# Log-sum rows of a windowed attention: one product and a masked spread on VectorE, or four products and plain copies on ScalarE

## The chip, the cores and the metric

The kernel runs on one core of a Trainium2 chip. A core has TensorE (PE in the profile, its weight loads PEld), VectorE (DVE), ScalarE (ACT), GpSimd (POOL) and SyncE (SP, which only issues transfers here). The metric is the device time of one execution in microseconds; the median over several executions counts.

## The reference

Two attention layers over 2048 tokens with 1024 features and 32 heads of 32 features each, in float32. Layer A attends to 8 tokens at a stride of 2, layer B to the last 256 tokens. Their outputs stand side by side. Cut to layer B, which the change touches:

```python
qkv = (x @ wqkv).reshape(B, S, 3, H, Dh)          # S = 2048, H = 32, Dh = 32
scores = einsum("bhqd,bhkd->bhqk", q, k) * Dh ** -0.5
mask = (i - j >= 0) & (i - j < 256)
p = softmax(where(mask, scores, -1e9))
o = einsum("bhqk,bhkd->bhqd", p, v)
return o.reshape(B, S, D) @ wo
```

## The kernel before

**Units and groups.** The work is cut into 8 units of 512 tokens: four "dense" ones of layer B, then four of layer A. A unit has 8 groups of 4 heads, so there are 32 dense groups. Every float32 operand of the large products is split into a high fp32r part and the rest, and each product is three matmuls (high by high, high by rest, rest by high).

**Stages of a dense group** (`qk_items` and `attention`). The projections for q and k run on TensorE (L586), ScalarE and VectorE split the result (L523, L527), and transfers of SyncE stack the parts in `qst` and `kst`, on partitions 0 to 95. Partitions 96 to 127 are free for the log-sum. `first` (L1089) makes scores with queries on the partitions, 16 tiles a group (4 blocks of 128 queries by 4 heads); VectorE adds the mask and takes the maximum (L1094), ScalarE takes the exponential with its sum (L1099), whose result is thrown away. After 16 tiles `log_sum` takes the logarithm on ScalarE (L1112), and `parts` forms minus maximum minus logarithm on VectorE (L1117) and splits it into `hl`, 128 queries by 2 parts by 16 tiles (L1119, L1120). `rows` transposes `hl` on TensorE by a product with the identity (L1128). `spread` writes the rows into partitions 96 to 127 of `qst` (L1134). `second` (L1172) then makes the scores once more, transposed, over all 128 partitions: the extra rows subtract the log-sum, so that the exponential (L1179) gives finished probabilities in `pbuf`. Masks set what lies outside the window to zero, on GpSimd (L1158) or VectorE (L1161). `values` (L1219) multiplies with v.

**The rows before the change.** The product of L1128 has `hl` as weights, 128 by 32, and gives 32 rows of 128 queries: row 16a + 4j + b holds part a of head j in block b. `spread` runs once for each head j. It repeats these rows over the 4 blocks (32 by 512) and multiplies by `pick`, a pattern that keeps in block b only the rows 4j + b and 16 + 4j + b. In `kst`, partitions 96 to 127 hold ones for all heads (`ones`, L413, once at the start), so `second` sums the rows that `pick` has left.

**What sets the order.** Instructions are written out by a planner in the kernel. `Clock` holds an estimated time for each engine; `ck.use` adds an operation, `ck.defer` puts a function off until a planned time. A loop at the end (L1285 on) takes the item that can start first in TensorE's plan, out of four sequences: log-sum rows (`aux`), `second` and `values` (`twos`), `first` (`ones`), and the projections (`gemm`). On a tie that order decides. An item has an estimated cost on TensorE, 0.08 for the rows. The planner also chooses the engine: casts of weights (L218 ScalarE, L221 VectorE), evictions (L607, L610) and masks (L1158, L1161) go where its estimate ends first. So another estimate moves other instructions. On the chip each engine runs its list in the planner's order and waits on semaphores.

**Banks and buffers.** Scores and rows share four PSUM banks (`rs`), taken in turn; a bank is free again after L1099, L1179 or L1134. Projections have three banks (`rg`), the values one. `qst` and `kst` have two buffers each, for alternate groups. GpSimd also issues the loads of weights (L173), each after the VectorE split that frees its buffer.

Of the kernel before, what the change touches and what calls it, by code (L numbers as in the profile page):

```python
# [7 lines left out]
F32 = mybir.dt.float32  # L8
F32R = mybir.dt.float32r
AF = mybir.ActivationFunctionType  # L10
ALU = mybir.AluOpType
# [3 lines left out]
P = 128  # L15
# [28 lines left out]
BANK_LATE = 0.0  # L44
# [189 lines left out]
def kernel(ctx, tc, xs, wqk, wv, wo, outs, units):  # L234


    nc = tc.nc
# [10 lines left out]
    pickp = ctx.enter_context(tc.tile_pool(name="pickp", bufs=1))  # L248
# [9 lines left out]
    ck = Clock()  # L258
# [113 lines left out]
    qst = [stackp.tile([P, 4, S], F32R, tag=f"q{i}", name=f"qst{i}") for i in range(2)]  # L372
    kst = [stackp.tile([P, 4, 256 + S], F32R, tag=f"k{i}", name=f"kst{i}") for i in range(2)]

    cst = {}

    def constants():
        def bands(name, n, keep, fill, *conds):
            m = const.tile([P, n], F32, name=name) if isinstance(name, str) else name
            nc.gpsimd.memset(m, keep)  # L380
            for step, base, chan in conds:
                nc.gpsimd.affine_select(m, m, pattern=[[step, n]], compare_op=ALU.is_ge, fill=fill, base=base,
                                        channel_multiplier=chan)
            return m

        ident = cst["ident"] = const.tile([P, P], F32R, name="ident")
        keep = const.tile([P, P], F32, name="keep_d")
        nc.gpsimd.memset(keep, 0.0)
        nc.gpsimd.affine_select(ident, keep, pattern=[[-1, P]], compare_op=ALU.not_equal, fill=1.0, base=0,
                                channel_multiplier=1)  # L390
        pick = cst["pick"] = pickp.tile([32, 16], F32, name="pick")
        nc.gpsimd.memset(pick, 0.0)
        for row in (0, 16):
            nc.gpsimd.affine_select(pick, pick, pattern=[[-1, 16]], compare_op=ALU.not_equal, fill=1.0, base=-row,
                                    channel_multiplier=1)
        cst["mask_d"] = bands("mask_d", 384, 0.0, FAR, (1, -1, -1), (-1, 256, 1))
        near = cst["near"] = band0[:, :200].rearrange("p (v c) -> p v c", v=5)
        nc.gpsimd.memset(near, 0.0)
        for i in range(4):
            part = near[32 * i:32 * i + 32]  # L400
            for step, base, chan in ((1, -1, -1), (-1, 8, 1)):
                nc.gpsimd.affine_select(part, part, pattern=[[0, 5], [step, 40]], compare_op=ALU.is_ge, fill=FAR,
                                        base=base, channel_multiplier=chan)
        nc.gpsimd.affine_select(near[0:32, 0, :], near[0:32, 0, :], pattern=[[1, 40]], compare_op=ALU.is_ge, fill=FAR,
                                base=-8, channel_multiplier=0)
        cst["keep_f"] = bands("keep_f", P, BIG, 0.0, (-1, -1, 1))
        cst["keep_d"] = bands(keep, P, BIG, 0.0, (1, 0, -1))
        ck.use("pool", 3.0, ck.now)

        def ones():  # L410
            zero = cst["mask_d"][96:P, None, P:2 * P].to_broadcast([32, 24, P])
            for t in kst:
                nc.scalar.activation(t[96:P, :, :].rearrange("p j (a s) -> p (j a) s", s=P), zero, AF.Identity,  # L413
                                     bias=1.0, scale=1.0)
                ck.use("act", 2.7, ck.now)

        ck.defer(24.0, ones)

    pfree = [0.0]
# [7 lines left out]
    xt, xready, ot, rows, waiting = {}, {}, {}, {}, {}  # L427
# [24 lines left out]
    rg, rs, ro = Ring(psg, 7 - NS, "g"), Ring(pss, NS, "s"), Ring(pso, 1, "o")  # L452
# [7 lines left out]
    def latest(*ts):  # L460
        return None if any(t is None for t in ts) else max(ts)
# [420 lines left out]
    def x_items(u):  # L882
        xt[u], xready[u] = [], []

        def run(g):
            a, b = st.get(where["x", u, g])
            xt[u] += a
            xready[u] += b

        return [[(lambda: 0.0, lambda g=g: run(g), 0.0, lambda: None)] for g in range(4)]  # L890
# [175 lines left out]
    def attention(u, s):  # L1066
# [5 lines left out]
        q, kk = qst[buf], kst[buf]  # L1072
# [37 lines left out]
        def log_sum():  # L1110
            ln = small.tile([P, 16], F32, tag="ln", name="ln")
            nc.scalar.activation(ln, h["sm"], AF.Ln)  # L1112
            e = ck.use("act", 0.13, ck.now) - 0.03

            def parts():
                nl = small.tile([P, 16], F32, tag="nl", name="nl")
                nc.vector.tensor_tensor(nl, h["nm"], ln, op=ALU.subtract)  # L1117
                hl = small.tile([P, 2, 16], F32R, tag="hl", name="hl")
                nc.vector.tensor_copy(hl[:, 0, :], nl)  # L1119
                nc.vector.tensor_tensor(hl[:, 1, :], nl, hl[:, 0, :].bitcast(F32), op=ALU.subtract)  # L1120
                e2 = ck.use("dve", 0.52, e, port=True)
                aux.append(Item(lambda: latest(rs.when(BANK_LATE), e2), lambda: rows(hl), 0.08))

            ck.defer(e, parts)

        def rows(hl):
            ps, bank = rs.take()
            nc.tensor.matmul(ps[0:32, 0:P], hl.rearrange("p a b -> p (a b)"), cst["ident"], start=True, stop=True)  # L1128

            def spread():  # L1130

                h["rows"] = []
                for j in range(4):
                    nc.vector.tensor_tensor(q[96:P, j, :].rearrange("p (b s) -> p b s", s=P),  # L1134
                                            ps[0:32, None, 0:P].to_broadcast([32, 4, P]),
                                            cst["pick"][0:32, 4 * j:4 * j + 4, None].to_broadcast([32, 4, P]), op=ALU.mult)
                    e = ck.use("dve", 0.61, ck.now)
                    h["rows"].append(e + ROWS_LATE)
                rs.give(bank, e)

            return spread
# [102 lines left out]
    aux, ones, twos, gemm = [], [], [], []  # L1244
    for u in range(U):
        for s in range(NG):
            a, b = attention(u, s)
# [3 lines left out]
    for p in plan:  # L1251
        if p[0] == "qk":
            new = qk_items(p[1], p[2])
            if p == ("qk", 0, 0):
                q, k, x = new[:NK], new[NK:], x_items(0)
# [16 lines left out]
    gemm = [Item(r, lambda run=run, after=after: (run(), after)[1], c) for r, run, c, after in gemm]  # L1272

    ck.defer(0.0, constants)
    if WARM:
        idle = qst[1][:, 0, :]
        nc.vector.memset(idle.bitcast(F32), 0.0)
        ps, bank = rs.take()
# [6 lines left out]
    while True:  # L1285
# [3 lines left out]
        for name, seq in seqs.items():  # L1289
# [3 lines left out]
            t = seq[pos[name]].ready()  # L1293
# [4 lines left out]
        if ck.later and (best is None or ck.later[0][0] < best[0]):  # L1298
            t = ck.later[0][0]
# [3 lines left out]
        t, name = best  # L1303
# [52 lines left out]
```

## Time and profile before

| | |
|---|---|
| median of 3 runs | 1816.4 us (1812.44 to 1818.7) |
| the profiled execution | 1818.1 us |
| its span, first to last instruction | 1816.4 us |
| granted clock of TensorE, mean | 0.995 |
| L1128, product for the rows | 32, mean 223 ns |
| L1134, spread on VectorE | 128, mean 676 ns, 79.3 us busy |
| L1099, exponential of the first pass, 128 by 384 | 448, mean 557 ns |
| L586, projection products, 128 by 512 | 3072, 773.0 us busy |

A row of a group reads: line, engine, operation, result and operands, shapes and count, then busy time, mean duration and the idle time of that engine just before, with what ended it. In a list of waits stand the total in us, the number of waits and the longest. A product's duration runs from its start to its modelled end and overlaps the next one. All lines L are of the kernel before unless it is said otherwise; in the changed kernel the lines from 393 on have numbers up to four higher.

### The profile page before, as it was taken

To read this page: it belongs to the slowest core of one execution; us is meant where nothing else is said; L and a number is where in the kernel's file an instruction comes from. 1 tells how busy PE (TensorE), PEld (TensorE's weight loads), DVE (VectorE), ACT (ScalarE), POOL (GpSimd) and SP (SyncE) were. 2 spreads that over 40 slices of the span, in tenths; PEclk is the share of its full clock that TensorE was granted. 3 is DMA by queue.
4 is the path that set the end of the run, shared out by engine and by line. 5 is a ranking of instruction groups with operands and counts; after the bars stand their busy time and mean duration, and the time that the engine had idled before them with its cause. 6 is when DMAs were issued, how large, how long until landed. Compare 5 with 4: busy or idle time off the path is not lost.

```text
span 1816.4 us, 38617 instructions
## 1 busy us (share of the span) xinstructions
PE 1789.4 (99%) x14730; PEld 1465.3 (81%) x14730; DVE 1262.0 (69%) x2790; ACT 924.4 (51%) x2301; POOL 410.1 (23%) x950
## 2 busy tenths in 40 slices
PE   9999999999999999999999999999999999999999
PEld 6787878888777788778887788888888887888887
DVE  6677876768867769777677566646755766557866
ACT  5556466555655565656555344423542544446342
POOL 2313323222242223333224300101010011002220
PEclk9999999999999999999999999999999999999999
DMA  7354664544646555454545343536753674348984
GB/s 239 114 142 136 183 168 139 167 139 137 183 139 177 146 144 170 134 166 128 160 110 164 106 150 119 164 123 213 249 173 113 221 250 137 120 144 297 311 265 145
DMA packets 129241, 303.61 MB, mean 167 GB/s; under 512 B 16160, under 2 KB 31520, under 8 KB 129056
## 3 DMA queue, kind: packets, MB, share of 16 engines
q0 software_dynamic: 45216, 164.65, 28.7%
q1 hardware_dynamic: 73472, 116.56, 22.8%
q10 hardware_dynamic: 10368, 19.93, 3.0%
q8 instruction: 117, 1.92, 0.4%
q14 instruction: 68, 0.56, 0.1%
HBM read 189.79 MB, written 44.04 MB: 129 GB/s over the span
## 4 chain that ended last, share of the span: by engine, by line
PE 91%; DMA 3%; ACT 2%; DVE 2%; issue 1%; SPq 0%; POOL 0%; ACTq 0%; DVEq 0%; POOLq 0%
PE g L586 37%; PE g L654 18%; PE g L714 10%; PE g L773 8%; PE s L1172 5%; PE s L1089 5%; PE o L1219 5%; PE s L923 2%; PE o L984 2%; DMA r<-od 2%; DMA raw<-xs 1%; ACT wide L970 1%; ACT s L1099 0%; DVE w L224 0%; DVE r L846 0%
## 5 line engine op out<-in xcount | busy, mean ns | idle before, releaser
L586 PE MATMUL g<-x,w 128*128 128x512 f32 x3072 | 773.0, 396 | 2.8 <-ACT x L218 2.6
L586 PEld LDWEIGHTS g<-x,w 128*128 128x128 f32 x3072 | 568.1, 189 | 114.5 <-issue 6.8
L654 PE MATMUL g<-w,x 128*128 128x256 f32 (+1 forms) x2304 | 393.7, 322 | 0.5 <-issue 0.3
L224 DVE TENSOR_TENSOR w<-raw,w 128x512 fp32r<-128x512 f32 x518 | 339.4, 697 | 51.8 <-ACT w L218 45.1
L654 PEld LDWEIGHTS g<-w,x 128*128 128x128 f32 x2304 | 334.5, 192 | 28.8 <-issue 1.6
L1099 ACT ACTIVATE s<-s,nm 128x384 f32<-128x384 f32 (+2 forms) x512 | 274.4, 537 | 101.8 <-DVE nm L1094 101.6
L1094 DVE CUSTOM_DVE_ANT_0 s<-s,mask_d 128x384 f32<-128x384 f32 (+2 forms) x512 | 261.7, 554 | 88.1 <-PE s L1089 87.4
L1158 POOL TENSOR_SCALAR_AFFINE_SELECT pbuf<-pbuf 128x128 f32<-128x128 f32 (+1 forms) x606 | 220.1, 391 | 326.2 <-ACT pbuf L1179 324.8
L1179 ACT ACTIVATE pbuf<-s 128x384 f32<-128x384 f32 (+2 forms) x480 | 202.8, 505 | 73.7 <-PE s L1172 72.1
L714 PE MATMUL g<-r,w 128*128 128x512 f32 x768 | 190.8, 394 | 1.4 <-ACT r L1054 0.7
L173 POOL DMA_DIRECT2D raw<-wqk x126 | 68.6, 545 | 440.8 <-DVE w L224 303.0
L714 PEld LDWEIGHTS g<-r,w 128*128 128x128 f32 x768 | 141.9, 188 | 30.7 <-DVE r L1058 1.6
L773 PE MATMUL g<-x,w 128*128 128x512 f32 x672 | 153.2, 390 | 0.5 <-DVE w L224 0.5
L773 PEld LDWEIGHTS g<-x,w 128*128 128x128 f32 x672 | 126.0, 188 | 27.3 <-DVE w L224 0.9
L221 DVE CAST w<-raw 128x1024 fp32r<-128x1024 f32 x187 | 129.3, 692 | 25.2 <-PE g L586 22.6
L1172 PEld LDWEIGHTS s<-qst,kst 128*128 128x128 f32 x704 | 113.3, 189 | 40.6 <-ACT s L1099 16.2
L1089 PE MATMUL s<-kst,qst 96*128 96x384 f32 (+2 forms) x512 | 142.5, 342 | 0.9 <-ACT s L1099 0.7
L1172 PE MATMUL s<-qst,kst 128*128 128x256 f32 (+2 forms) x704 | 136.4, 302 | 3.5 <-ACT s L1099 3.0
L1089 PEld LDWEIGHTS s<-kst,qst 96*128 96x128 f32 x512 | 93.5, 189 | 25.8 <-issue 3.9
L931 DVE TENSOR_TENSOR band<-s,near 128x160 f32<-128x160 f32 x128 | 32.5, 316 | 116.0 <-PE s L923 116.0
L1099 ACT ACTIVATION_READ_ACCUMULATOR s<-s,nm 128x1 f32 x512 | 105.4, 206 | 0.0
L970 ACT COPY wide<-band 32x512 f32<-32x512 f32 x128 | 79.0, 618 | 49.2 <-DVE band L961 47.2
(81 smaller groups left out, 1405.7 us busy)
## 6 DMA issues: line engine op xcount, KB each, us to landing
raw<-wqk POOLq DMA_DIRECT2D x126, 512.0 KB, 4.3
raw<-wv POOLq DMA_DIRECT2D x72, 512.0 KB, 4.9
qst<-nat SPq DMA_DIRECT2D x96, 256.0 KB, 5.4
kst<-nat SPq DMA_DIRECT2D x96, 256.0 KB, 5.5
raw<-wo POOLq DMA_DIRECT2D x44, 512.0 KB, 4.4
raw<-xs POOLq DMA_DIRECT2D x28, 512.0 KB, 4.5
outs<-ost ACTq DMA_DIRECT2D x37, 256.0 KB, 2.8
kst<-halo SPq DMA_DIRECT2D x72, 128.0 KB, 4.4
```

What stands on the lines that cost most here:

```text
L221: nc.vector.tensor_copy(t[:, 0, :], raw)
L224: nc.vector.tensor_tensor(t[:, 1, c:c + 512], raw[:, c:c + 512], t[:, 0, c:c + 512].bitcast(F32), op=ALU.subtract)
L586: nc.tensor.matmul(h["ps"], h["w"][:, a, k * P:(k + 1) * P], xt[u][k][:, b, :], start=(k == 0 and i == 0), stop=(k == NK - 1 and i == 2))
L654: nc.tensor.matmul(ps, xt[u][kw * g + k][:, a, p0:p0 + P], h["w"][g][:, c, k], start=(first and t == 0 and half == 0), stop=(last and t == 2),
L714: nc.tensor.matmul(h["ps"], w[:, a, c:c + P], ot[u, k][:, b, :], start=(k == 0 and i == 0), stop=(k == NK - 1 and i == 2))
L773: nc.tensor.matmul(h["ps"], w[:, a, c:c + P], x[:, b, :], start=(k == 0 and t == 0), stop=(k == 3 and t == 2))
L1089: nc.tensor.matmul(ps[:, :n], q[0:96, j, b * P:(b + 1) * P], kk[0:96, j, c0:c1], start=True, stop=True)
L1094: nc.vector.tensor_tensor_reduce(ps[:, :n], ps[:, :n], mask[:, cut:full], scale=-1.0, scalar=BIG, op0=ALU.add, op1=ALU.min, accum_out=nm)
L1099: nc.scalar.activation(ps[:, :n], ps[:, :n], AF.Exp, bias=nm, scale=-1.0, accum_out=sm)
L1158: nc.gpsimd.affine_select(w, w, pattern=[[0, m], [step, n]], compare_op=ALU.is_ge, fill=0.0, base=base, channel_multiplier=chan)
L1172: nc.tensor.matmul(ps[:, i * n:(i + 1) * n], kk[:, j, 256 + kb * P:256 + (kb + 1) * P], q[:, j, q0:q0 + n], start=True, stop=True)
L1179: nc.scalar.activation(w, ps[:, :pack * n].rearrange("p (j n) -> p j n", j=pack), AF.Exp)
```

## The change

`pick` becomes a tile of 128 partitions; in its partitions 96 to 127 and first 4 columns it holds a one where the row is j or 4 + j in column j. The head's pattern is put into `kst` with it: `ones` adds column j of `pick` to zeros for head j, so only rows 96 + j and 100 + j are one there. Partitions 96 to 127 of both `qst` are set to zero once by GpSimd. `rows` makes four products, one for each block b, each with the 8 columns (part a, head j) of that block as weights; they fill 8 rows by 512 queries of one bank. `spread` copies these 8 rows to partitions 96 to 103 of `qst`, the same for each of the four heads, on ScalarE. The planner's costs change with it: 0.28 for the products, 0.485 on ScalarE for a copy in place of 0.61 on VectorE.

```diff
-        pick = cst["pick"] = pickp.tile([32, 16], F32, name="pick")
+        pick = cst["pick"] = pickp.tile([P, 16], F32, name="pick")
         nc.gpsimd.memset(pick, 0.0)
-        for row in (0, 16):
-            nc.gpsimd.affine_select(pick, pick, pattern=[[-1, 16]], compare_op=ALU.not_equal, fill=1.0, base=-row,
+        part = pick[96:P, :4]
+        for row in (0, 4):
+            nc.gpsimd.affine_select(part, part, pattern=[[-1, 4]], compare_op=ALU.not_equal, fill=1.0, base=-row,
                                     channel_multiplier=1)
...
         def ones():
-            zero = cst["mask_d"][96:P, None, P:2 * P].to_broadcast([32, 24, P])
-            for t in kst:
-                nc.scalar.activation(t[96:P, :, :].rearrange("p j (a s) -> p (j a) s", s=P), zero, AF.Identity,
-                                     bias=1.0, scale=1.0)
-                ck.use("act", 2.7, ck.now)
+            zero = cst["mask_d"][96:P, None, P:2 * P].to_broadcast([32, 6, P])
+            for t, qs in zip(kst, qst):
+                nc.gpsimd.memset(qs[96:P].bitcast(F32), 0.0)
+                ck.use("pool", 1.8, ck.now)
+                for j in range(4):
+                    nc.scalar.activation(t[96:P, j, :].rearrange("p (a s) -> p a s", s=P), zero, AF.Identity,
+                                         bias=cst["pick"][96:P, j:j + 1], scale=1.0)
+                    ck.use("act", 0.7, ck.now)
...
-                aux.append(Item(lambda: latest(rs.when(BANK_LATE), e2), lambda: rows(hl), 0.08))
+                aux.append(Item(lambda: latest(rs.when(BANK_LATE), e2), lambda: rows(hl), 0.28))
...
-            nc.tensor.matmul(ps[0:32, 0:P], hl.rearrange("p a b -> p (a b)"), cst["ident"], start=True, stop=True)
+            for b in range(4):
+                nc.tensor.matmul(ps[0:8, P * b:P * b + P], hl.rearrange("p a (j b) -> p a j b", b=4)[:, :, :, b],
+                                 cst["ident"], start=True, stop=True)
...
                 for j in range(4):
-                    nc.vector.tensor_tensor(q[96:P, j, :].rearrange("p (b s) -> p b s", s=P),
-                                            ps[0:32, None, 0:P].to_broadcast([32, 4, P]),
-                                            cst["pick"][0:32, 4 * j:4 * j + 4, None].to_broadcast([32, 4, P]), op=ALU.mult)
-                    e = ck.use("dve", 0.61, ck.now)
+                    nc.scalar.copy(q[96:104, j, :], ps[0:8, :])
+                    e = ck.use("act", 0.485, ck.now)
```

## The prediction

> **What bounds the kernel now.** I read the page first, then the busy time by stretches, then the waits of TensorE. The page: span, engines, chain.
>
> ```profile
> span 1816.4 us, 38617 instructions
> PE 1789.4 (99%) x14730; PEld 1465.3 (81%) x14730; DVE 1262.0 (69%) x2790; ACT 924.4 (51%) x2301; POOL 410.1 (23%) x950
> PE 91%; DMA 3%; ACT 2%; DVE 2%; issue 1%; SPq 0%; POOL 0%; ACTq 0%; DVEq 0%; POOLq 0%
> ```
>
> TensorE is the bound: busy for 99% of the span and 91% of the chain that ended last. VectorE, from which the change takes work, is 69% busy and makes 2% of the chain. The change touches the dense units alone, so I cut the span at the first scores and at the last log-sum row (columns: window, its length, then busy us of each engine, granted clock, DMA).
>
> ```profile
> 24.00:1015.00 991.00, 983.34 (x5966) 796.42 (x5965) 745.38 (x1926) 579.51 (x1676) 298.75 (x735) 1.00 0.54 152
> 1015.00:1816.40 801.40, 786.38 (x8706) 654.53 (x8704) 505.86 (x849) 336.05 (x612) 101.67 (x186) 1.00 0.56 185
> ```
>
> In the dense stretch TensorE is busy for 983.3 of 991.0 us: 7.7 us idle. ScalarE is 58% busy there (579.5/991), VectorE 75%. Whose fault the idle time is, the waits of TensorE in that window say; two waits of the weight loads and the first of ScalarE's follow.
>
> ```profile
> PE s L1172 <- ACT s L1099: 3.0, 4, 1.1
> PE s L1128 <- DVE hl L1120: 2.6, 3, 2.0
> PE s L1089 <- ACT s L1099: 0.7, 1, 0.7
> PE g L714 <- DVE r L1058: 0.5, 2, 0.2
> PE s L1172 <- ACT pbuf L1179: 0.3, 1, 0.3
> PE g L654 <- DVE w L224: 0.2, 1, 0.2
> ```
>
> ```profile
> PEld s L1172 <- ACT s L1099: 16.2, 26, 1.6
> ...
> PEld s L1128 <- ACT ln L1112: 3.8, 3, 2.4
> ```
>
> ```profile
> ACT s L1099 <- DVE nm L1094: 101.6, 104, 5.5
> ```
>
> Twelve waits, 7.3 us. The largest are for score banks that the exponentials (L1099) give back and for hl, the log-sum halves; none is for the spread rows of L1134. The weight loads wait 16.2 us for the same banks, most of it beneath a running product. ScalarE's exponentials themselves wait 101.6 us for VectorE's maxima. So all that a faster side engine can give back in the dense stretch is some 7 us and what hangs on it. One thing does: the longest wait, 2.0 us.
>
> ```profile
> 178.00:180.50 2.50, 0.51 (x4) 0.10 (x3) 1.22 (x4) 1.64 (x6) 0.00 (x0) 1.00 1.06 214
> 180.50:184.00 3.50, 3.50 (x17) 3.50 (x18) 3.22 (x6) 0.84 (x2) 0.00 (x0) 0.51 1.06 238
> ```
>
> Behind it the granted clock is 0.51 for 3.5 us, which costs 3.5 x 0.49 = 1.7 us more. Waits and clock: 9.0 us.
>
> **The change part by part: the products.** One product of 32 weight columns becomes four of 8, each with 128 moving columns, in 32 groups: 96 more products, all on TensorE, which has next to no idle time. Their price: the timeline at one of them, and the group of products with 128 moving columns and full weights.
>
> ```profile
> 465.25 0.22 PE L1128 MATMUL s<-ident,hl 128*32 128x128 f32 x1 [0.31 <-DVE hl L1120]
> 465.25 0.53 PEld L586 LDWEIGHTS g<-x,w 128*128 128x128 f32 x3
> 465.31 0.91 PE L586 MATMUL g<-x,w 128*128 128x512 f32 x3
> ```
>
> ```profile
> L1172 PE MATMUL s<-qst,kst 128*128 128x128 f32 x224 | 36.3, 260 | 2.2 <-ACT s L1099 1.8 <-ACT pbuf L1179 0.3
> ```
>
> The product is shown as 0.22 us long, but the next starts 0.06 us after it: products overlap, and what one takes of TensorE's time is that step. Three more a group: 3 x 0.06 x 32 = **5.8 us**, all on the path. From above: the 224 products with full weights are busy 36.3 us, 0.162 each, so 3 x 0.162 x 32 = 15.6 us; from below, 0, if every group's products fall into a wait that is there anyway. I take 5.8, since L1128 is the same product with the same moving operand, and eight weight columns are no more to load than 32.
>
> [...] The trace has a single product here and never four in a row, so no row settles it.
>
> **The spread.** The four VectorE instructions of a group go.
>
> ```profile
> L1134 DVE TENSOR_TENSOR qst<-s,pick 32x512 fp32r<-32x512 f32 x128 | 79.3, 676 | 9.9 <-PE s L1128 9.3
> ```
>
> VectorE loses 79.3 us. Four ScalarE copies from PSUM to an fp32r tile take their place, of 8 partitions and 512 elements. The rows nearest to them:
>
> ```profile
> L1054 ACT CAST r<-o 128x512 fp32r<-128x512 f32 x32 | 18.8, 587 | 38.5 <-PE o L1219 38.4
> L970 ACT COPY wide<-band 32x512 f32<-32x512 f32 x128 | 79.0, 618 | 49.2 <-DVE band L961 47.2
> L218 ACT CAST x<-raw 128x512 fp32r<-128x512 f32 x80 | 45.8, 618 | 53.6 <-DMA raw<-xs 21.5 <-DVE band L791 8.8 <-DMA outs<-ost 6.0
> L1179 ACT ACTIVATE pbuf<-s 128x512 f32<-128x512 f32 x112 | 65.1, 610 | 19.9 <-PE s L1172 18.7
> L1179 ACT ACTIVATE pbuf<-s 128x384 f32<-128x384 f32 x256 | 108.4, 507 | 38.6 <-PE s L1172 38.3
> ```
>
> ```profile
> 456.51 2.01 ACT L1179 ACTIVATE pbuf<-s 128x384 f32<-128x384 f32 x5
> ```
>
> A copy of 512 from PSUM takes 587 ns; 32 partitions (L970) cost the 618 of 128 (L218), so the 8 rows save nothing. In a row they overlap: five of 384 in 2.01 us step by (2.01 - 0.51)/4 = 0.38, and 512 add the 0.10 between 610 and 507: 0.48. A group's four last 3 x 0.48 + 0.59 = 2.0 us and hold ScalarE for 1.9; 32 groups: 62 us. In the order of the changed kernel nine evictions and two weight casts move from ScalarE to VectorE, and 26 masks from VectorE to GpSimd: the planner hands the new balance on. ScalarE rises to about 64% of the dense stretch and VectorE falls to about 67%. Neither becomes a bound on average, and neither is on the path: the cover is TensorE's products of the projections. I count nothing for it. Without that cover a group pays up to its 2.0 us (third rival).
>
> A new wait comes with it: the first copy waits for the fourth product, on ScalarE's queue. The old one waited on VectorE, 9.3 us in all as its row ends. Behind the copies stand, in the new order, exponentials L1099 in 6 groups, L1179 in 10 (which need the rows anyway), stores of outputs in 12, evictions in 4. TensorE has 6 or more projection products between the four and their first user in most groups, at least 1.4 us. I count nothing.
>
> **The start.** Two GpSimd memsets of 2048 elements go between weight loads; two fills of kst become eight.
>
> ```profile
> 24.60 0.73 POOL L173 DMA_DIRECT2D raw<-wv  x1 [11.11 <-DVE w L224]
> 27.45 0.70 POOL L173 DMA_DIRECT2D raw<-wv  x1 [2.12 <-DVE w L224]
> 29.38 0.72 POOL L173 DMA_DIRECT2D raw<-wv  x1 [1.22 <-DVE w L224]
> 38.90 0.70 POOL L173 DMA_DIRECT2D raw<-wv  x1 [8.80 <-DVE w L224]
> ```
>
> ```profile
> L1024 POOL MEMSET wide<- 128x2176 f32 x2 | 3.8, 1906 | 0.0
> L413 ACT ACTIVATE kst<-mask_d 32x3072 fp32r<-32x3072 f32 x2 | 5.4, 2762 | 0.0
> ```
>
> ```profile
> 33.86 0.34 ACT L1099 ACTIVATE s<-s,nm 128x128 f32<-128x128 f32 x1 [3.41 <-DVE nm L1094]
> 35.16 1.55 PE L654 MATMUL g<-w,x 128*128 128x512 f32 x6
> ```
>
> By L1024 a memset takes 1.8 us, so the pair runs from 25.3 to 28.9 and the load of 27.45 leaves 1.5 us late, that of 29.38 some 0.3; the next has 8.8 us of room. The products that use these weights begin at 35.16, with the earlier ones. The fills give about 0.6 us more, and ScalarE then idles 3.41. Nothing on the path. Without this cover it would be 1.5 us at most.
>
> **The sum.** The profiled execution took 1818.1 us, its span and 1.7 around it; +5.8 gives 1823.9. The median of the three runs shown is 1816.4, 1.7 lower, and it is what I predict against: 1816.4 + 5.8 = **1822**, +0.32%. About 0.3% (5.4 us) is what a measurement of this kernel can tell from no change, so the forecast stands on the border; with the bounds of the product its own span is 1818 to 1832.
>
> **The rivals.** *Hidden.* The products stand right where TensorE waits for hl (2.6 us, 3 times), and the copies end 0.4 us sooner than VectorE's four. That covers 3 groups of 32 by the row; to cover all, the new order must have waits there. Half of the cost: 1819. The change would then free VectorE and buy nothing.
>
> *VectorE was behind the waits* (the other side). hl is made on VectorE, and the 101.6 us that the exponentials wait is VectorE's too; a spread of 2.5 us no longer stands ahead of maxima. If all waits went, 7.3 + 1.7 (clock) + 12 x 0.15 for products that again overlap (0.22 - 0.06, as above) = 10.8 us: 1811 with the products at 5.8, 1806 with them at 0; I say 1809. It decides once VectorE's queue, not the order of banks, ends the waits. Against it: TensorE's idle time is a ceiling, and the products eat half of it.
>
> *ScalarE takes VectorE's place.* Copies ahead of exponentials keep score banks: in the 6 groups where L1099 is next, 2.0 us each is 12 us: 1816.4 + 5.8 + 12 = 1834. It decides where TensorE has less than 2 us of other products before its next bank. For it: banks from L1099 are already the first cause of waits. Against it: in 26 groups something else stands behind the copies, and the exponentials wait for VectorE far more than for anything on their own engine. One wait as long as that at 178 us would bring the half clock as well, 1.7 us as above. [...]
>
> **How the numbers follow.** Forecast 0.46 (1822; a little under half of it within 0.3%), hidden 0.16 (1819), VectorE behind the waits 0.16 (1809, mostly faster by over 0.3%, below 1811.0), ScalarE as new gate 0.22 (1834). Faster: 0.8 x 0.16 = 0.13. Same: 0.43 x 0.46 + 0.15 + 0.03 = 0.38. Slower: the rest, 0.49. The range leaves out half of each outer rival, 0.08 + 0.11: 1809 to 1834.
>
> **What the profile after would show.** Right: 128 products of L1133 about 0.06 us apart, TensorE's dense stretch longer by 5 to 7 us of busy time and its idle time still near 7; L1140 at 587 ns; no PE wait on L1140. Hidden: the stretch no longer. VectorE behind the waits: idle time under 3 us and no clock of 0.5. ScalarE as gate: waits on the exponentials for banks above 10 us. I am wrong if the dense stretch (24 to 1015) moves by less than 3 us or more than 16, or if the rest moves, whose order of instructions on TensorE is the same for its last 5447 of 11404 products.

## The result and the profile after

The changed kernel takes **1838.2 us**, median of five runs (1836.9 to 1842.0), against 1816.4 for the kernel before (1812.4 to 1818.7): a ratio of 1.0129, 95% interval 1.0110 to 1.0149. It is slower by 21.8 us; 1822 was predicted, with a range that ended at 1834. The profiled execution took 1836.9 us.

The page, in its parts for the span, the engines and the chain:

```profile
span 1835.2 us, 38771 instructions
PE 1797.9 (98%) x14826; PEld 1471.8 (80%) x14826; DVE 1183.3 (64%) x2647; ACT 982.9 (54%) x2424; POOL 417.9 (23%) x978
PE 90%; DVE 3%; DMA 3%; ACT 2%; issue 1%; SPq 0%; POOL 0%; ACTq 0%; DVEq 0%; POOLq 0%
```

TensorE is busy for 8.5 us more and still the bound, but the span grew by 18.8: the rest is TensorE standing. VectorE lost 78.7 us of work and ScalarE took on 58.5. The windows of the prediction:

```profile
24.00:1015.00 991.00, 977.24 (x5998) 791.85 (x5997) 661.34 (x1778) 633.26 (x1792) 298.89 (x756) 0.99 0.53 149
1015.00:1835.20 820.20, 800.61 (x8758) 665.27 (x8756) 508.51 (x849) 337.87 (x617) 106.50 (x192) 0.99 0.56 183
176.40:183.20 6.80, 5.56 (x20) 5.09 (x20) 3.10 (x5) 5.32 (x11) 2.57 (x6) 0.50 0.88 195
```

In the dense stretch TensorE's idle time went from 7.7 to 13.8 us, and the place near 180 us where the clock is halved lasts 6.8 us, not 3.5. A second place of halved clock is new:

```profile
207.10:210.50 3.40, 3.40 (x10) 2.75 (x9) 2.56 (x6) 1.14 (x5) 0.72 (x1) 0.50 1.06 257
```

The two operations that are new, from the groups, and one place of them on ScalarE's timeline:

```profile
L1133 PE MATMUL s<-ident,hl 128*8 128x128 f32 x128 | 12.8, 222 | 6.0 <-DVE hl L1124 6.0
L1140 ACT CAST qst<-s 8x512 fp32r<-8x512 f32 x128 | 64.3, 571 | 51.2 <-PE s L1133 50.9
```

```profile
469.13 2.01 ACT L1140 CAST qst<-s 8x512 fp32r<-8x512 f32 x4 [1.29 <-PE s L1133]
```

Both have their predicted size: the products start 0.055 to 0.064 us apart, the copies are 571 ns each and four in a row take 2.0 us. TensorE's waits in the window of 24 to 1016 us, and two of the weight loads' list, show what is new:

```profile
PE s L1133 <- DVE hl L1124: 6.0, 5, 1.9
PE s L1093 <- ACT s L1103: 4.6, 5, 1.2
PE s L1176 <- ACT qst L1140: 1.4, 1, 1.4
PE s L1176 <- ACT pbuf L1183: 0.3, 1, 0.3
PE g L658 <- DVE w L224: 0.2, 1, 0.2
```

```profile
PEld s L1093 <- ACT s L1103: 11.8, 23, 1.7
...
PEld s L1176 <- ACT qst L1140: 2.2, 3, 1.6
```

TensorE waits for the new copies once. What grew are old waits: hl from 2.6 to 6.0, banks of the first pass from 0.7 to 4.6 on TensorE and from 3.8 to 11.8 on its weight loads; this is the row of the kernel before:

```profile
PEld s L1089 <- ACT s L1099: 3.8, 15, 1.0
```

TensorE's waits for the banks of the second pass (L1172, now L1176), 3.0 us before, are gone. In the later dense units the new waits recur at the same places, 260 us apart: near 462, 722 and 982 us for a bank, near 496 and 756 for hl. ScalarE and TensorE at the first place of the one kind, then VectorE and TensorE at the first of the other:

```profile
461.52 0.60 ACT L527 ACTIVATE nat<-g 128x512 fp32r<-128x512 f32 x1 [3.72 <-PE g L590]
462.01 0.55 ACT L1103 ACTIVATE s<-s,nm 128x384 f32<-128x384 f32 x1
```

```profile
462.73 2.13 PE L1093 MATMUL s<-kst,qst 96*128 96x384 f32 x4 [1.25 <-ACT s L1103]
```

```profile
493.32 0.69 DVE L221 CAST w<-raw 128x1024 fp32r<-128x1024 f32 x1 [1.54 <-PE g L658]
494.05 1.29 DVE L224 TENSOR_TENSOR w<-raw,w 128x512 fp32r<-128x512 f32 x2
495.26 0.17 DVE L1121 TENSOR_TENSOR nl<-nm,ln 128x16 f32<-128x16 f32 x1
```

```profile
495.99 0.40 PE L1133 MATMUL s<-ident,hl 128*8 128x128 f32 x4 [1.35 <-DVE hl L1124]
```

At 461 us a projection copy, which waits for TensorE, stands on ScalarE's queue ahead of an exponential; TensorE then waits for the bank that this exponential gives back. At 493 us a weight cast, which waits for TensorE too, stands ahead of the log-sum parts. The order of the queues has changed with the planner's costs, and at these places a waiting instruction (3.72 us on ScalarE, 1.54 on VectorE) held what stood behind it.

To say where the time went I took the step from each product's start to the next and subtracted the median step of its kind in the kernel before. With two profiles of each kernel (the second pair is the last experiment's), the means differ by 23.5 us: 5.9 for the added products; 8.8 of excess over those medians (97.7 to 106.5) up to the last product of weights and values (L1223) of the dense units; 5.6 (18.3 to 23.9) from there to the last 5447 products, where the order differs still; and 3.2 (36.3 to 39.4) in those last ones, whose order is the same.

The 8.8 fit waits and clock. TensorE's waits between 24 and 1016 us sum to 12.5 and 12.0 us in the two profiles of the changed kernel, 7.3 and 7.2 in those of the kernel before: 5.0 more. The clock is halved there for 10.2 us in each profile of the changed kernel, for 3.4 in one of the kernel before and not at all in the other. At a granted clock of 0.50 half of that length is lost where TensorE has work throughout, so at most 4.3 us more.

### The profile page after: what moved, and what is told of

It is laid out like the page before. It is cut to its first block, busy times and chain, and to the rows that moved or that the text cites. A ratio compares the mean times of both kernels' runs of the same rounds, so it can differ in the third digit from the quotient of the medians.

```text
span 1835.2 us, 38771 instructions
## 1 busy us (share of the span) xinstructions
PE 1797.9 (98%) x14826; PEld 1471.8 (80%) x14826; DVE 1183.3 (64%) x2647; ACT 982.9 (54%) x2424; POOL 417.9 (23%) x978
## 4 chain that ended last, share of the span: by engine, by line
PE 90%; DVE 3%; DMA 3%; ACT 2%; issue 1%; SPq 0%; POOL 0%; ACTq 0%; DVEq 0%; POOLq 0%
PE g L590 37%; PE g L658 16%; PE g L718 10%; PE g L777 8%; PE s L1176 6%; PE s L1093 5%; PE o L1223 4%; PE s L927 2%; PE o L988 2%; DMA raw<-xs 2%; DMA r<-od 1%; DVE w L224 1%; PE s L1133 0%; ACT wide L974 0%; DVE s L1098 0%
## 5 line engine op out<-in xcount | busy, mean ns | idle before, releaser
L1093 PE MATMUL s<-kst,qst 96*128 96x384 f32 (+2 forms) x512 | 144.5, 342 | 5.7 <-ACT s L1103 4.6
L1176 PEld LDWEIGHTS s<-qst,kst 128*128 128x128 f32 x704 | 110.2, 190 | 38.6 <-ACT s L1103 14.8
L1176 PE MATMUL s<-qst,kst 128*128 128x256 f32 (+2 forms) x704 | 134.5, 305 | 1.8 <-ACT qst L1140 1.4
L1093 PEld LDWEIGHTS s<-kst,qst 96*128 96x128 f32 x512 | 93.4, 189 | 31.4 <-ACT s L1103 11.8
L173 POOL DMA_DIRECT2D raw<-wv x72 | 46.6, 647 | 295.9 <-DVE w L224 195.8
```

The costliest lines, as they stand in the source:

```text
L1093: nc.tensor.matmul(ps[:, :n], q[0:96, j, b * P:(b + 1) * P], kk[0:96, j, c0:c1], start=True, stop=True)
L1176: nc.tensor.matmul(ps[:, i * n:(i + 1) * n], kk[:, j, 256 + kb * P:256 + (kb + 1) * P], q[:, j, q0:q0 + n], start=True, stop=True)
```

## The experiments

The kernel before took 1815.3 to 1816.4 us on the chips used. Two theories stood at first: the loss is the **order** that the planner makes of the new costs; or it is the **copies on ScalarE** themselves. The first three runs part instructions from order; a fourth doubles the products. Lines added to a kernel shift its line numbers; where a view below has other numbers, the text says what they are.

**new_ops_old_order2**: the changed kernel's instructions, charged to the planner as the old ones were, so that everything else stays where it was.

```diff
-                aux.append(Item(..., lambda: rows(hl), 0.28))
+                aux.append(Item(..., lambda: rows(hl), 0.08))
...
                     nc.scalar.copy(q[96:104, j, :], ps[0:8, :])
-                    e = ck.use("act", 0.485, ck.now)
+                    e = ck.use("dve", 0.61, ck.now)
```

> The changed kernel's products, copies and key pattern, with the planner charged as before the change, so that every other instruction stands in the order of the kernel before. Order theory (the new order of the queues makes most of the loss): the products' 5.9 us and little more, 1820 to 1825 us, waits of the first scores for banks near those of before (0.7 us). Rival, ScalarE theory (the copies on ScalarE hold the exponentials up): 1832 or more, since the copies stand in ScalarE's queue at places that were not planned for them. Rival, price theory (the products cost more than their steps): above 1832 without new waits.

**products_only_old_order2**: the same with the copies on VectorE.

```diff
-                    nc.scalar.copy(q[96:104, j, :], ps[0:8, :])
+                    nc.vector.tensor_copy(q[96:104, j, :], ps[0:8, :])
```

> As the first run, but the four copies of a group are plain copies on VectorE at the place of the old spread: the products and the key pattern alone, in the old order. Order theory and price by steps: 1820 to 1824 us. ScalarE theory: the same 1820 to 1824, and the first run at least 8 us above it. If the two agree within 3 us, the copies on ScalarE cost nothing in the old order.

**old_ops_new_order2**: the kernel before with the changed kernel's charges (0.28 for rows, 0.485 on ScalarE for the spread, the fills in their parts), so in the changed kernel's order.

> The old product and the spread on VectorE, with the planner charged as after the change, so that every other instruction stands in the order of the changed kernel. Order theory: the loss stays but for the products, 1828 to 1834 us, with the waits at 461, 721 and 981 us in place. ScalarE theory: back to 1816 to 1820, since nothing is copied on ScalarE.

**products_twice2**: eight products a group in the changed kernel, in its order.

```diff
-            for b in range(4):
+            for b in [i % 4 for i in range(8)]:
```

> The changed kernel with each of the four products issued twice, order and charges unchanged: 128 more products. Price by steps of 0.06 us: +7.7 us over the changed kernel, 1844 to 1848. If products fall into waits: +0 to 4. If a product costs 0.16: +20, near 1858.

**copies_on_vector_new_order**, run later, is the last corner of the table below: the changed kernel with the second diff above and its own charges.

> The changed kernel with its four copies as plain copies on VectorE at the same place, and the planner's charges as they are, so that every other instruction keeps the changed kernel's order. Theory (in this order the copies on ScalarE are paid for by the order, which costs 17.8 us with the old instructions too): the old instructions in this order 1833.4, plus 5.9 for the products, so 1836 to 1842, no faster than the changed kernel. Rival (ScalarE's time is what costs in this order too): 10 us or more faster than the changed kernel, 1824 to 1830.

Measured, medians in us, with the 95% interval of the ratio to the kernel before:

| | order before | order of the changed kernel |
|---|---|---|
| old instructions | 1815.6 | 1833.4 (1.0079 to 1.0119) |
| four products, copies on VectorE | 1821.5 (1.0021 to 1.0051) | 1834.8 (1.0078 to 1.0133) |
| four products, copies on ScalarE | 1836.1 (1.0099 to 1.0132) | 1838.2 (1.0110 to 1.0149) |

products_twice2: 1848.6 (1.0165 to 1.0210), 10.5 over the changed kernel for 128 products, 0.08 each; their own step accounts for 7.7 of it. That is 0.6 above the range of the price by steps, and far from the other two.

Both theories hold, and they do not add up. new_ops_old_order2 (1836.1) came out where the ScalarE theory had it and the order theory did not; old_ops_new_order2 (1833.4) the other way round. In the old order the products cost 5.9, as predicted, and the copies on ScalarE 14.6 more. The new order spares 11 of those 14.6, but it costs 17.8 with the old instructions, which did not need it. In it the products add 1.4 and the copies on ScalarE 3.4, which the intervals do not tell from nothing; products_twice2, in the same order, shows that products are not free in it. Its corner on VectorE, 1834.8, lies a little below what the order theory gave and far above the rival. What the copies do in the old order is in the waits of new_ops_old_order2:

```profile
PE s L1175 <- ACT qst L1139: 3.4, 4, 0.9
...
PE s L1092 <- ACT qst L1139: 2.6, 5, 0.5
```

TensorE waits for the copies themselves (L1139 here; L1092 and L1175 are the scores of the first and second pass), nine times, 6.0 us in all; its weight loads wait for them 10.5 us, in part at the same time. The waits for banks of the exponentials are those of before (3.0 and 0.6 us): what is late are the rows. The changed kernel's order does away with most of this wait. In the profiles 10.5 us of the copies' price lie before the last 5447 products and 4.1 in them (531.2 us against 527.1 with the copies on VectorE), a part that is taken up below.

**Other orders of the same instructions.** One charge is changed in each: the rows' 0.08 to 0.28 in the kernel before (old_ops_rows_charge); 0.28 to 0.24 in the changed one (new_ops_rows_024); and its charge for a product of 512 columns (new_ops_charge_0227).

```diff
-C1, C3, CG, CV = 0.108, 0.2, 0.231, 0.242
+C1, C3, CG, CV = 0.108, 0.2, 0.227, 0.238
```

> The kernel before, with one number changed: the planner's charge for the log-sum product on TensorE, 0.08 to 0.28 us. Every instruction is that of before; some of the products stand in another order. Theory (orders that the planner makes differ by many us at the same work): the time leaves before's by more than 5 us, to either side, 1821 to 1835 us the likelier. Rival (what costs is ScalarE's new work, an order alone costs nothing): 1813 to 1819 us.

> The changed kernel with one number changed: the planner's charge for the four log-sum products, 0.28 to 0.24 us. Every instruction is that of the changed kernel; a few products stand in another order. Theory (orders differ by many us at the same work): off the changed kernel's 1838 us by 3 us or more, likelier to the fast side since its order has five known bad places, 1828 to 1835 us. Rival (ScalarE's new work costs, whatever the order): 1836 to 1840 us.

> The changed kernel with two numbers changed: the planner's charges for a product of 512 columns, 0.231 and 0.242 us to 0.227 and 0.238, nearer to the 0.227 us between starts that the traces show. Every instruction is that of the changed kernel, in another order from early on. Theory (orders differ by many us at the same work, and a planner whose clock is nearer to the chip's puts fewer waiting instructions ahead of ready ones): 1822 to 1834 us. Rival (ScalarE's new work costs, whatever the order): 1835 to 1841 us.

Measured: 1827.5 (1.0047 to 1.0077), 1839.8 (1.0105 to 1.0148), 1838.5 (1.0102 to 1.0163). The first is 12 us lost by an order alone, as the theory had it. The other two are misses, and came out where the rival had them: no other order that a charge made of the new instructions is faster. So the old instructions came to 1815.6, 1827.5 and 1833.4 in three orders, the new ones to 1836.1, 1838.2, 1838.5 and 1839.8 in four. Of the three the order of the kernel before is the best for the old instructions, and both changes of costs leave it.

**five_places_swapped**: the changed kernel; three projection copies (near 461, 721 and 981 us) go behind the next two exponentials, and two weight splits (494, 754 us) behind the log-sum parts. TensorE's order is untouched.

```diff
+HOLD_SPLIT, HOLD_NAT = (76, 113), (16, 24, 32)
...
-            nc.scalar.activation(hl[:, 0, :], ps, AF.Copy, scale=sc)
+            do(lambda: nc.scalar.activation(hl[:, 0, :], ps, AF.Copy, scale=sc))
...
                     nc.scalar.activation(ps[:, :n], ps[:, :n], AF.Exp, bias=nm, scale=-1.0, accum_out=sm)
+                    HELD["left"] -= 1
+                    if HELD["left"] <= 0:
+                        let_go("nat")
```

> The changed kernel with the emission of five things put back by a few places on their own engine's queue, and nothing else moved: the three projection copies L527, L527 and L486 that stand ahead of ready exponentials near 461, 721 and 981 us go behind the next two exponentials (their DMAs with them), and the two weight splits (cast L221 and its two L224) ahead of the log-sum parts near 494 and 754 us go behind those parts. TensorE's order and VectorE's and ScalarE's other work are the same. Theory (the loss is an order of the in-order queues that puts a waiting instruction ahead of a ready one): TensorE's waits of 1.25 + 3 x 0.39 us in L1093 go at three places and of 1.35 us in L1133 at two, 10.5 us, so about 1828 us (1825 to 1831). Rival (a wait that goes is only taken up by the next, since the copies and splits are late themselves now): 1835 to 1839 us.

Measured: 1833.4 (1.0087 to 1.0128), 4.8 below the changed kernel, between the two ranges expected; the intervals of the two kernels overlap, so the timelines must show what happened. One of the three places of a bank on TensorE's timeline, in the changed kernel and then in this one (L1115 is its L1093):

```profile
722.64 2.13 PE L1093 MATMUL s<-kst,qst 96*128 96x384 f32 x4 [1.25 <-ACT s L1103]
```

```profile
722.77 1.01 PE L1115 MATMUL s<-kst,qst 96*128 96x384 f32 x2 [0.61 <-ACT s L1125]
```

The mechanism is shown at four of the five places: TensorE gains 1.5 us at 496 and at 756, 0.9 at 722 and 1.1 at 982. At 461 it loses 1.8: a load landed 0.8 us later, two waits of 0.50 and 0.61 us stand there in place of one of 1.25, and behind them the clock is halved. The size was overrated, 3.2 us net of 10.5: once the exponential is free to go, it waits for VectorE's maxima instead, as ScalarE's timeline shows at 461 (L1125 is the exponential, L1120 the maximum).

```profile
464.80:468.20 3.40, 3.40 (x9) 2.73 (x10) 3.33 (x14) 1.95 (x8) 0.72 (x1) 0.50 0.39 111
```

```profile
461.76 0.56 ACT L1125 ACTIVATE s<-s,nm 128x384 f32<-128x384 f32 x1 [3.96 <-DVE nm L1120]
```

The profile is 6.9 shorter than the changed kernel's, but 2.7 of that lie in the last 5447 products, whose order is the same.

**What ScalarE's time costs in the old order.** The kernel before, with work added that is no part of the computation: five copies of a constant a group (two, in spare_copies_two), which wait for nothing and which nobody reads; and five that read the log-sum product's bank (spare_copies_of_rows).

```diff
                     e = ck.use("dve", 0.61, ck.now)
+                    for _ in range(2 if j == 3 else 1):
+                        nc.scalar.copy(cst["spare"].rearrange("p (b s) -> p b s", s=P),
+                                       cst["ident"][0:8, None, :].bitcast(F32).to_broadcast([8, 3, P]))
```

> The kernel before with work added that is not part of the computation: at the place where VectorE spreads the log-sum row, ScalarE makes five copies of a constant of 8 x 384 elements into a tile that nobody reads (five of 384 instead of four of 512, as the room on the chip allows no more), with no charge, so that every other instruction keeps its order. The spread stays on VectorE. They take ScalarE's queue for about the time of the changed kernel's four copies (2.00 us a group), but wait for nothing and nobody waits for them. Theory (the price of the copies in the old order, 14.6 us, is that TensorE waits for rows that arrive late, behind ScalarE's queue): 0 to 5 us over before, 1816 to 1821. Rival (it is ScalarE's time as such, which pushes every later exponential): 8 to 15 us over before, 1824 to 1831.

> The kernel before with two spare copies of a constant on ScalarE a group in place of five, that nobody reads and nobody waits for: 0.9 us of its queue a group instead of 2.2. Theory (the price rises with ScalarE's time): two fifths of the 18 us of the five, 1821 to 1825 us. Rival (ScalarE has slack up to some point and the first copies are free): 1814 to 1819 us.

> The same, but the five spare copies read the product of the log-sum step in its PSUM bank, so that ScalarE's queue also stands until TensorE has made the product, and the bank comes free only behind them; still nobody waits for what they write, and the spread that the second scores wait for stays on VectorE. Theory (late rows): as in the run above, at most a few us more for the bank, 1816 to 1823. Second theory (the wait at the head of ScalarE's queue holds ready exponentials behind it): 5 to 12 us more than the run above. Rival (ScalarE's time as such): the same as the run above, 1824 to 1831.

Measured: five 1833.3 (1.0076 to 1.0112), two 1823.5 (1.0027 to 1.0072), 18.1 and 7.2 over before. The theory that only late rows cost fell with the first, since nobody reads these copies; the price is above the rival's range too. The price rises with ScalarE's time, by the medians two fifths of it for two fifths of the copies. The window of 24 to 1016 us in spare_copies_alone, three of its waits (L1090 and L1100 are product and exponential of the first pass, L1176 the product of the second, L1135 the spread), and one group of the copies:

```profile
24.00:1016.00 992.00, 975.18 (x5915) 786.47 (x5914) 735.78 (x1906) 645.40 (x1812) 298.09 (x732) 1.00 0.55 150
```

```profile
PE s L1090 <- ACT s L1100: 5.8, 4, 1.8
PE s L1176 <- ACT s L1100: 4.2, 7, 1.1
...
PE s L1176 <- DVE qst L1135: 2.1, 4, 0.8
```

```profile
469.86 2.67 ACT L1140 CAST spare<-ident 8x384 bf16<-8x384 f32 x5
```

ScalarE is 65% busy there, and TensorE's waits for the exponentials' banks in the first pass are 5.8 us, not 0.7; it also waits 2.1 us for the spread, for which it did not wait before. This execution was the fastest of its kernel, 1828.2 us, and its waits grew by 9.2 us in all: they account for most of its own 10.1, not for the 18.1 of the medians. With two copies the waits grew by 0.9 only (8.2 against 7.3), but the clock is halved for 13.6 us in that window in place of 3.4, at most 5.1 us; so the two fifths are no proof that one mechanism grows in step with the copies.

Five copies hold ScalarE 2.7 us a group, 86 us in all, so by the medians TensorE pays about a fifth of their length; by the same measure the changed kernel's copies, 2.0 us a group and 64 in all, paid 14.6 in the old order, 0.23, though there the waits shown are for late rows. spare_copies_of_rows gave 1938.8 (1.0657 to 1.0699), far above all three of its ranges, and tells nothing of what it was made for: ScalarE's and VectorE's reads of the one bank were made to wait for each other in turn, as the timelines of both show.

```profile
51.09 0.47 ACT L1140 CAST spare<-s 8x384 bf16<-8x384 f32 x1 [0.42 <-DVE qst L1135]
52.31 0.47 ACT L1140 CAST spare<-s 8x384 bf16<-8x384 f32 x1 [0.75 <-DVE qst L1135]
```

```profile
51.59 0.68 DVE L1135 TENSOR_TENSOR qst<-s,pick 32x512 fp32r<-32x512 f32 x1 [0.54 <-ACT spare L1140]
52.80 0.68 DVE L1135 TENSOR_TENSOR qst<-s,pick 32x512 fp32r<-32x512 f32 x1 [0.53 <-ACT spare L1140]
```

**Second profiles**, for the stretch behind the dense units:

> The changed kernel once more, for a second profile. Of the 18.7 us between the first two profiles 7.2 lay in the sparse stretch, whose instructions are the same in the same order. Theory (that part is chance of one execution): its excess over the steps' medians comes out anywhere from 56 to 63 us. Rival (it belongs to the changed kernel): 62 to 64 us again.

> The kernel before once more, for a second profile. Theory (chance of one execution): the excess of the sparse stretch comes out anywhere from 55 to 63 us. Rival (it belongs to the kernel): 55 to 57 us again.

The excess there came to 63.6 after 63.0 in the changed kernel and to 53.3 after 55.8 in the one before: the changed kernel repeats itself, as the rival had it, and the one before came out below both ranges. So the difference is not chance as far as two executions of each can tell. Divided as above, 5.6 of it lies where the order still differs. The 3.2 in the last 5447 products stay **open**: their excess runs from 33.7 to 46.6 us over all kernels here, and no run was made for it; in the first profiles the clock is halved there for 6.8 us before and 10.2 us after the change, and TensorE waits 1.4 us for a transfer after it, while the list of its waits before shows none. They are no fixed part of the changed kernel: products_twice2 and five_places_swapped, with the same products there, take 528.1 and 528.8 us for them, the kernel before 528.3, the changed kernel 531.5.

No version beats the kernel before.

## Why the prediction was wrong

*The products: right.* 5.8 us was predicted; the steps sum to 5.7 and 5.9 in the two profiles, and products_only_old_order2 is 5.9 slower. The range of 1818 to 1832 given for the products alone has a slip: with a price of nothing it begins at 1816. Four in a row start 0.055 to 0.064 us apart at 128 moving columns.

*The spread: the step that failed.* "Neither becomes a bound on average, and neither is on the path: the cover is TensorE's products of the projections. I count nothing for it." The duration was right (2.0 us a group), and so were the shares (ScalarE 64%, VectorE 67%); the count of nothing was not. In the old order it is 14.6 us, of which the trace shows TensorE waiting 6.0 for the copies themselves and 4.1 in the last products, which stay open; the spare copies show that ScalarE's time cost 18.1 us even where nobody read what it made, though it was busy for 65% of the dense stretch. An average says nothing of who waits for the next instruction. The step passed over the planner in one sentence ("the planner hands the new balance on"); its new order alone is 17.8 us. It takes away most of the new wait and makes others. The loss of the kernel as planned is this order's: with the copies back on VectorE it stays (1834.8).

*The new wait on ScalarE: counted at nothing, too little.* In the changed kernel ScalarE stands 50.9 us ahead of its copies for the products (VectorE stood 9.3 before its spread). TensorE waits for the copies once, 1.4 us, where the prediction had no such wait; in the old order 6.0. No run parts this wait from the copies' own time: spare_copies_of_rows was meant for it and tells nothing.

*The halved clock: no term in the sum.* The prediction took 1.7 us of it to hang on the longest wait, 2.0 us. The second profile of the kernel before has the same wait without it, and in the changed kernel 3.4 us of halved clock stand behind waits of 0.36 and 0.50 us. What sets it off stays open.

*The start: right.* In the first 60 us TensorE has no new wait above 0.2 us.

*The rivals.* Hidden and "VectorE was behind the waits" are out: with 84 us less work for VectorE in the dense stretch (745.4 to 661.3) the kernel is slower, and the waits for hl grew. No run took work from VectorE without giving it to ScalarE, so what that alone is worth was not measured. "ScalarE takes VectorE's place" was nearest, 1834, by luck: its price came from log-sum copies ahead of exponentials (in the trace such an exponential is ScalarE's next work in 10 groups, not 6), while at the places found in the kernel as planned it is projection copies that stand ahead of exponentials. Its own sign, more than 10 us of TensorE waiting for banks, did not appear (4.6).

*The sign for being wrong* appeared, since the rest moved: the last 5447 products take 3.2 us longer. The cut at 1015 us tells less than was thought: the last log-sum row comes only 1.0 us later (1013.0 to 1014.0), because the new order has left 48 projection products for afterwards; at the first of the last 5447 the kernel is 15.6 us later (1288.1 to 1303.7). Twelve waits of 7.3 us in the profile before were read as the most that could be gained; that the order which left so few could be lost had no term in the sum.

## What to carry to other kernels

A planner that is fed costs turns any change of an operation's engine or length into another order of every queue, so price the order as a term of its own and separate it by experiment: new instructions with old charges, old instructions with new charges. An engine at 58% was not free here: its queue gives back the buffers of the bound engine, and work added to it cost about a fifth of its length by the medians (18.1 of 86 us). And take a second profile of the same kernel before hanging a cost on one wait in the first.

## What the runs showed of the hardware that was not expected

- The plain copy of 8 by 512 from PSUM on VectorE (L1140 in copies_on_vector_new_order) is as long as the multiplication of 32 by 512 that it replaces, 676 ns; on ScalarE it is 571, close to the 587 of 128 rows:

```profile
L1140 DVE CAST qst<-s 8x512 fp32r<-8x512 f32 x128 | 79.3, 676 | 22.2 <-PE s L1133 22.0
```

- Five copies of 8 by 384 from SBUF to bf16 step by (2.67 - 0.51)/4 = 0.54 us on ScalarE, more than the 0.48 of 8 by 512 from PSUM to fp32r.
- Two waits of 1.95 us (175.1) and 1.38 us (177.6) stand around the start of the halved clock at 176.4; it lasted 6.8 us, against 3.5 in the kernel before with one wait of 2.0 us. Yet the wait alone did not bring it: the second profile of the kernel before has the same wait at the same instruction, with a granted clock of 1.00 behind it. TensorE in the first profile, then in the second; the twelve products behind the wait take 2.84 and 1.64 us:

```profile
180.44 0.23 PE L1128 MATMUL s<-ident,hl 128*32 128x128 f32 x1 [1.99 <-DVE hl L1120]
180.50 2.84 PE L654 MATMUL g<-w,x 128*128 128x256 f32 x12
```

```profile
178.29 0.22 PE L1128 MATMUL s<-ident,hl 128*32 128x128 f32 x1 [1.99 <-DVE hl L1120]
178.35 1.64 PE L654 MATMUL g<-w,x 128*128 128x256 f32 x12
```
